# Five products of constants on the whole TensorE array, placed between the tasks of a recurrent-attention and MLP kernel

## The chip, the cores and the metric

One core of a Trainium2 chip runs the kernel. The metric is the device time of one execution in microseconds. The engines are TensorE (PE; its weight loads are listed apart as PEld), VectorE (DVE), ScalarE (ACT), GpSimd (POOL), and SyncE (SP), which issues the transfers. Each works through its own queue of instructions in order and waits on semaphores for the others.

## What is computed

The input is six arrays of 4 batches, 8 heads, 768 time steps and 40 channels. A recurrent state of 40 by 40 per batch and head is read and updated step by step; the outputs of all heads are put side by side and go through an MLP with a gated activation.

```python
for t in range(S):
    y[:, :, t] = einsum('bhd,bhde->bhe', r_t, state)
    Sa = einsum('bhde,bhe->bhd', state, a_t)
    state = state * w_t[:, :, None, :] - einsum('bhd,bhe->bhde', Sa, b_t)
    state = state + einsum('bhd,bhe->bhde', v_t, k_t)
x = y.transpose(0, 2, 1, 3).reshape(3072, 320)
h = x @ w_in                                # 320 -> 2048
out = (h * sigmoid(1.702 * h)) @ w_out      # 2048 -> 320
```

## The kernel before

The 768 steps are cut into 12 chunks of 64, and the 4 batches into 2 pairs. One chunk of one pair is a **unit**; there are 24, numbered from 0. Units 0 and 1 are the first chunk of the two pairs, 2 and 3 the second, and so on. Within a chunk the recurrence is solved as a triangular system, so that nearly all work is matrix products. For each unit the code makes these stages:

- `decay`: logarithms of w are summed by two products into `ps_cum` and `ps_cumc` (in the first four units), and ScalarE takes exponentials of them (FT, GT, wch, G).
- `prep`: the inputs are scaled by these; two products give the scores `ps_A` and `ps_RV`, which VectorE masks into A and RV.
- `inverse`: one product gives the scores `ps_N`; then five levels double the inverse of a triangular block. In the first four units this is `plain_level`: TensorE makes `ps_level` from EX and PT (40 instructions, the last eight with the identity tile `ident`), ScalarE or VectorE copies it into PT (L784), VectorE transposes it into EX (L723), and the next level takes both. After the last level come T (L707), `ps_Q`, and `ps_T`, which fill in the lower block.
- `solve`: from unit 2 on the carried state is turned over (`ps_zT`) and read (`ps_rz`); `ps_B` collects the known side, `ps_X` applies the inverse, VectorE masks it into M (L907), and `ps_y` adds the products of RV with kh and of M with bh: alternating groups of eight instructions, 64 in all. The result goes out to memory and comes back turned (`x_dram`, `xT_all`) for the MLP.
- `mlp`, one for each chunk (both pairs): `up` tasks into `ps_up`, an activation into g, `down` tasks into `ps_down`. The weights are put together from pieces in the first 75 us (L447 to L463).

Nearly all products work on a quarter of the 128x128 array (64 rows by 64 columns). Four such products run side by side on the four quarters, and each float32 product is two weight loads and two matmul instructions in the profile. All are recorded by the helper `mm` at L300.

Every step is a task. `Plan.add` records which tasks it must follow; the order of all tasks on all engines is written out by hand in the string `ORDER` and put into effect by `listed`. A token names a task by number, engine (p TensorE, a ScalarE, d VectorE, g GpSimd, s SyncE), and for those that use PSUM the bank pair 0 to 3. A tile in PSUM is made by `psum` for the pair of the token; the tasks that share a tile form a chain, and the next tile on the same bank pair has to wait until the one before it has been read. The order of tokens of one engine is the order in its queue.

On TensorE the order around the change is this, with the tokens: unit 0's level 0 (107p0), its level 1 (110p3), ps_N and ps_RV of unit 1, further levels of units 0 and 1 mixed with ps_cum and ps_cumc of unit 2, unit 0's last level (119p3), unit 0's ps_Q (126p2), ps_N of unit 2, a level of unit 1, ps_T and ps_X of unit 0, unit 1's last level, unit 0's ps_y (136p1), unit 1's ps_Q (182p0), ps_B of unit 1, ps_A of unit 2, ps_T of unit 1, a level and ps_RV of unit 2, unit 1's ps_X (190p0), ps_cum and ps_cumc of unit 3 (334p1, 335p3), unit 1's ps_y (192p2), ps_zT of unit 2 (316p0), unit 2's level 1 (295p3), unit 3's ps_N (358p1), unit 2's level 2 (298p3), ps_rz of unit 2, ps_RV of unit 3, two levels, ps_zT, another level, ps_B, a level, ps_A, ps_cum, and then the first `up` tasks. From there on the tasks of later units stand between `up` and `down` tasks.

Of the kernel before, what the change touches and what calls it, by code (L numbers as in the profile page):

```python
# [108 lines left out]
4a 11s 132p0 104a1 105d1 142p2 26s 143p3 133a0 106d 130p1 14s 144a3 13s 107p0 15s 18s 151g 108a0 109d0 51s 131a1 110p3 27s  # L109
149g 150d 111a3 112d3 159p0 156p1 145a2 161d0 160a0 152g 113p3 345s 92a 162d 25s 153d 114a3 163p2 42s 115d3 34s 19a 274s 264p0  # L110
165d2 265p3 164a2 22d 266a3 166p2 20d 273s 21d 33s 43s 167a2 154p3 168d2 23g 35s 28a 157d1 116p2 155d3 169p1 117a2 118d2 267a0
279d 63s 280g 119p3 277s 171d1 36s 44s 123a3 120d3 343s 125d3 121a 278g 124d3 29d 287a 126p2 170a1 288p0 127a2 30d 172p1 122a3
31d 289a0 128p2 54s 173a1 129d2 32g 174d1 134p3 147s 37a 290d0 175p2 135d3 180a2 146s 178a2 275s 176d2 136p1 179a2 479s 38d
181a2 45s 39d 177a 282g 291d 91s 138a1 182p0 188p3 281d 183a0 186p2 139d 137a1 283p0 187a2 184p1 189a3 40d 276s 292p2 46a
284d0 41g 285p3 185d1 344s 148a 286d3 190p0 293a2 294d2 334p1 335p3 357a 140s 191d0 268g 336a3 315d 192p2 47d 337a1 348d 316p0
194a2 295p3 349d 61s 317a0 195g 60s 347s 358p1 296a3 62s 297d3 360d1 318a0 298p3 271a 361d 319p0 338g 300d3 196s 193a2 320a0
346s 355p2 385d 270s 48d 299a3 362p0 356d2 351g 301p3 363a0 364d0 350g 269s 141s 386p2 197s 302d3 365p0 387a2 352g 359a1 303d3
388a2 323p1 367d0 366a0 321p3 49d 324a1 304p2 322a3 478s 325d1 50g 353p0 309a2 470p3 354d0 209p1 307a2 210p1 310a2 305d2 211p1
308a2 272d 198p0 341a 199p0 72s 212p1 70s 64a 200p0 340s 368p2 52s 342d 339s 69s 201p0 369a2 202p0 370d2 203p0 471a 213p1 65d
214p1 389p2 66d 472a3 483g 204p0 390a2 560s 371p3 67d 306a 53s 215p1 71s 482s 216p1 372a3 217p1 476a 220p2 373d3 68g 218p1  # L120
221p2 477d 219a1 205p0 222p2 206p0 223p2 224p2 207p0 55a 311p3 225p2 79s 312d3 80s 226p2 208a0 58d 313p1 374p3 314d1 227p2 56d
379a3 228p2 229p2 57d 326p0 230a2 59g 393p1 327d0 378a3 391p2 394a1 375d3 231p0 558s 392d2 376a 232p0 233p0 395d1 559s 81s 73a
78s 234p0 480s 381p2 235p0 328p1 481s 382a2 74d 377a3 485d 380a3 236p0 75d 492a 242p2 486d 243p2 82a 76d 484d 77g 383p3 237p0
384d3 244p2 329d1 330d1 488p3 473d 238p0 531d 245p2 487g 246p2 489d3 85d 532p1 239p0 533a1 396p3 331d 332s 474s 475s 534a1
240p0 247p2 397d3 562s 241a0 535p1 83d 490p3 536a1 84d 398p0 572a 491d3 86g 550p1 555s 561s 253p3 399d0 551a 333s 400d0 254p3
401d 402s 554s 255p3 552a1 564d 493p0 705s 556a 567g 570p1 403s 494d0 248p2 563d 566g 249p2 495d0 498d 256p3 571d1 565g 250a2
496a0 251d2 252s 696p1 497g 557d 539p0 537p2 704s 257p3 538a2 540d0 258p3 553d 611d 697a 499d 573p2 784s 700s 259p3 576a2
574d2 710d 260p3 541d0 575d2 404p0 578d 261a3 577g 405p0 579d 698a1 568p2 711g 500p1 406p0 569d2 501a1 407p0 262d3 263s 708s
580p2 702a 502d1 408p0 582d2 409p0 503d 410p0 583d 504a 612p3 411p0 584g 613d3 412p0 614d3 413p0 505p1 709d 414a0 426p3 506d1
427p3 428p3 507d1 429p3 699d 581d2 430p3 615p1 785s 706s 701s 703d 431p3 616a1 585p0 432p3 508d 586a0 433p3 587d0 434p3 509a  # L130
588d 435p3 589d 448p2 436a3 510p1 590p0 511a1 449p2 592d0 591a0 512d1 415p3 513d 416p3 593d 514a 417p3 594g 418p3 515p0 419p3
516a0 517d0 595p1 518d 420p3 596a1 597d1 421p3 598d 422p3 519a 599d 423p3 424p3 520p0 425a3 437p1 521d0 438p1 523d0 522g 439p1
524d0 440p1 525d0 441p1 442p1 526d0 527p3 718p0 929s 528a3 443p1 719d0 787s 444p1 720d0 529p3 445p1 721d0 446p1 530d3 600p0
723d 447a1 542p3 722d 724g 603d0 605a0 619p1 604d0 543d3 450p2 620a1 606d0 544p3 621d1 601d0 602d 617p1 707s 546d3 451p2 618a1
783s 712d 547g 713d 607p0 725p1 608a0 452p2 609p0 453p2 548s 610d0 932s 454p2 727d1 726d1 622p0 728d 545d3 729a 775p1 455p2
623d0 780s 776a 549s 756d 730p3 624p0 456d2 457d2 731d3 458s 459p2 777a1 778g 732d3 786s 788g 781a 779s 626d0 460p2 625d0 627g
733d 795p1 835d 734a 461p2 735p3 791g 462p2 628s 736a3 796d1 737d3 716p0 792g 738d 463p2 782d 739g 1011s 920p1 757p3 925s
464p2 717d0 758a3 629s 759a3 790d 465p2 740p0 789d 466p2 741a0 742d0 921a 797p3 467d2 760p0 1008s 468d2 800a3 923d 652p2 469s
761d0 922a1 653p2 926a 930s 798d3 714p1 799d3 654p2 924s 802d 801g 655p2 934d 803a 656p2 836p0 657p2 715d1 658p2 659p2 837d0
762p3 838d0 927d 660p2 763a3 661p2 764p1 662a2 743d 630p0 744d 928s 631p0 632p0 765d1 804p3 766d1 633p0 805a3 806d3 634p0 807d  # L140
635p0 808a 745p2 636p0 748d2 637p0 749d2 839p1 933g 750d2 638p0 840a1 1009s 751d2 639p0 809p3 746d2 935g 640a0 641p1 810d3
642p1 793p2 747a 811d3 674p0 812d 794d2 813a 752p3 643p1 753a3 814p2 644p1 815a2 816d2 754p3 645p1 755d3 646p1 817d 647p1 818a
767p2 841p3 768d2 648p1 842a3 649p1 819p2 650p1 820a2 821d2 675p0 769p3 822d 651a1 823d 771d3 931s 770d3 772g 824p2 936d 676p0
827a2 828a2 942p1 829a2 677p0 1153s 830a2 937d 945a1 773s 663p3 825d2 664p3 943d1 1156s 826a 665p3 944d1 999p2 947d 946g 666p3
1000a 1004s 980d 940p1 948g 667p3 941d1 668p3 774s 669p3 670p3 831p1 671p3 1001a2 1002d 1003s 832d1 672p3 1005a 1013d 678p0
673a3 1006d 833p2 843p1 679p0 834d2 1007s 844d1 938p2 845d1 680p0 939d2 846p3 681p0 847d3 949p1 1012g 682d0 848p2 950a1 683d0
1014d 684s 685p3 849d2 1015g 1010s 850d2 1021p0 1016g 951d1 686p3 1024a0 1232s 851d 1235s 981p2 687p3 982a2 952d 852s 1022d0
983a2 953g 1144p1 1023d0 688p3 1026d 1145a 1149s 1025d 1027g 984p2 1059d 689p3 1154s 954p0 853s 985a2 1147g 690p3 1158d 1148s
955a0 956d0 986p2 1146a1 957d 1150a 691p3 958d 987a2 1151d 988p0 692p3 989a0 1152s 990d0 959p1 693a3 865p2 960a1 694d3 866p2
961d1 867p2 695s 962d 868p2 963d 1028p0 869p2 1029a0 1030d0 870p2 1031d 1157g 871p2 1159d 1032a 1060p3 872p2 873p2 1061a3  # L150
874p2 1062d3 1033p1 875a2 854p0 1035d1 855p0 1036d 856p0 1037d 1063p3 857p0 1064d3 1034a1 858p0 964p2 859p0 965a2 966d2 1038p1
# [97 lines left out]
def rwkv7_gelu_quick(ctx: ExitStack, tc: tile.TileContext, time_d, v_d, w_d, wc_d, ak_d, b_d, rv_d, w_in, w_out, out):  # L249
# [93 lines left out]
    ident = single("ident", [128, 64])  # L343
# [689 lines left out]
    for i in range(NU):  # L1033
# [10 lines left out]
        if i % 2:  # L1044
            mlp(i // 2)
# [84 lines left out]
```

## Time and profile before

| | us |
|---|---|
| runs shown, median (lowest to highest) | 678.83 (678.51 to 679.16) |
| the profiled execution's own time | 678.87 |
| its span in the profile | 677.2 |
| TensorE busy | 650.6 |
| VectorE, ScalarE, GpSimd busy | 447.1, 330.6, 175.0 |
| mean granted clock of TensorE | 0.989 |

The profile is one execution. It is read by its page (busy time, the span in 40 slices, the chain of work that ended last, the costliest groups) and by views of the trace: the timeline, which lists runs of like instructions with start and length in us, the count behind an x, and in brackets the idle time of the engine before them with what ended it; the view of stretches, which gives for each stretch how long the engine was busy and the clock that TensorE was granted (1.00 is full); and the chain of waits, in order of time. "issue" as releaser means that the profile shows nothing that the engine waited for.

### The profile page before, as it was taken

What the parts mean: (1) busy time and instruction counts of PE and PEld (TensorE: products, weight loads), DVE (VectorE), ACT (ScalarE), POOL (GpSimd) and SP (SyncE); (2) the same over time, 40 slices, a digit from 0 to 9 for tenths busy, and PEclk for the clock granted to TensorE, in tenths of its full rate; (3) what the DMA queues carried; (4) which work ended last, traced back from release to release, by engine and by line L of the source; (5) the groups of instructions that cost most, each with busy time, mean ns of one, the idle gap of its engine ahead of it and who ended that gap; (6) DMA issues with size and microseconds to landing.
All of it is one profiled execution on the core that took longest, in us unless ns stands there. A gap on an engine that the chain in (4) does not pass through costs nothing.

```text
span 677.2 us, 42176 instructions
## 1 busy us (share of the span) xinstructions
PE 650.6 (96%) x19488; PEld 561.3 (83%) x19488; DVE 447.1 (66%) x906; ACT 330.6 (49%) x688; POOL 175.0 (26%) x204
## 2 busy tenths in 40 slices
PE   5668999999999999999999999999999999999997
PEld 5567887987987888898998898787988799899895
DVE  5686887777768668667776687868556766675001
ACT  4675955634664655554545435454454354252110
POOL 6442444224123023124123211321412321300000
PEclk9887999999999999999999999999999999999999
DMA  7883736315324224332304413513412412100100
GB/s 234 295 252 126 235 111 183 103 45 157 111 64 132 84 62 129 106 107 77 113 24 133 139 34 108 155 33 107 145 34 72 126 46 63 53 14 29 45 12 20
DMA packets 35311, 69.72 MB, mean 103 GB/s; under 512 B 5440, under 2 KB 14656, under 8 KB 35136
## 3 DMA queue, kind: packets, MB, share of 16 engines
q1 hardware_dynamic: 35136, 67.03, 32.6%
q8 instruction: 153, 2.51, 1.5%
q14 instruction: 22, 0.18, 0.1%
HBM read 59.15 MB, written 7.86 MB: 99 GB/s over the span
## 4 chain that ended last, share of the span: by engine, by line
PE 94%; ACT 2%; DVE 2%; issue 1%; DMA 1%; DVEq 0%; ACTq 0%; SPq 0%
PE ps_up L300 31%; PE ps_down L300 31%; PE ps_level L300 9%; PE ps_y L300 5%; PE ps_B L300 5%; PE ps_X L300 2%; PE ps_A L300 2%; PE ps_rz L300 2%; PE ps_N L300 2%; PE ps_RV L300 2%; PE ps_zT L300 1%; ACT PT L784 1%; PE ps_cum L300 1%; PE ps_Q L300 1%; PE ps_T L300 1%
## 5 line engine op out<-in xcount | busy, mean ns | idle before, releaser
L300 PE MATMUL ps_up<-xT_all,w_sb 64*64 64x256 f32 x3840 | 250.1, 377 | 0.4 <-PE ps_rz L300 0.2
L300 PE MATMUL ps_down<-w_sb,g 64*64 64x320 f32 x3072 | 239.5, 430 | 0.3 <-ACT zr L869 0.2
L300 PEld LDWEIGHTS ps_up<-xT_all,w_sb 64*64 64x64 f32 x3840 | 169.6, 133 | 15.3 <-issue 0.8
L300 PEld LDWEIGHTS ps_down<-w_sb,g 64*64 64x64 f32 x3072 | 133.3, 133 | 39.8 <-issue 1.3
L988 ACT ACTIVATE g<-ps_up 128x1024 f32<-128x1024 f32 x48 | 49.2, 1024 | 45.0 <-PE ps_up L300 44.6
L709 POOL TENSOR_TENSOR EX<-ES,quads 128x512 f32<-128x512 f32 x29 | 38.3, 1323 | 113.3 <-DVE ES L702 75.8
L751 ACT COPY W<-ps_level 128x512 f32<-128x512 f32 x56 | 32.7, 585 | 69.7 <-PE ps_level L300 68.0
L300 PEld LDWEIGHTS ps_level<-W,EX 64*64 64x64 f32 x2560 | 58.7, 134 | 5.8 <-DVE T L830 0.2
L300 PE MATMUL ps_level<-W,EX 64*64 64x64 f32 (+1 forms) x2560 | 55.9, 217 | 0.0
L753 DVE TENSOR_TENSOR E<-two,ps_level 128x256 f32<-128x256 f32 x80 | 33.2, 416 | 34.0 <-ACT W L751 30.3
L707 ACT ACTIVATE EX<-ES,quads 128x256 f32<-128x256 f32 x80 | 36.3, 501 | 30.5 <-DVE ES L702 29.9
L619 POOL TENSOR_TENSOR ak<-ak,FT 128x512 f32<-128x512 f32 x16 | 21.4, 1335 | 75.9 <-DMA ak<-in_ak 52.0
L300 PEld LDWEIGHTS ps_level<-PT,EX 64*64 64x64 f32 x1280 | 32.1, 146 | 8.8 <-DVE EX L723 5.7
L300 PE MATMUL ps_level<-PT,EX 64*64 64x64 f32 (+2 forms) x1280 | 34.2, 245 | 5.3 <-DVE EX L723 4.5
L702 DVE STREAM_TRANSPOSE ES<-E 128x256 f32<-128x256 f32 x80 | 35.3, 443 | 4.4
L300 PE MATMUL ps_y<-M,bh 64*64 64x104 f32 (+1 forms) x768 | 35.0, 247 | 2.4 <-issue 2.1
L300 PE MATMUL ps_y<-RV,kh 64*64 64x104 f32 (+1 forms) x768 | 34.8, 247 | 0.0
L891 ACT COPY B<-ps_B 128x416 f32<-128x416 f32 (+1 forms) x34 | 16.5, 491 | 33.8 <-PE ps_B L300 33.6
L300 PEld LDWEIGHTS ps_y<-RV,kh 64*64 64x64 f32 x768 | 28.5, 133 | 2.3 <-DVE M L907 0.5
L300 PEld LDWEIGHTS ps_y<-M,bh 64*64 64x64 f32 x768 | 27.2, 133 | 2.8 <-issue 2.3
L907 DVE TENSOR_TENSOR M<-ps_X,later 128x832 f32<-128x832 f32 (+1 forms) x24 | 23.8, 993 | 8.2 <-PE ps_X L300 8.0
L627 POOL TENSOR_TENSOR kh<-time,G 128x320 f32<-128x320 f32 x18 | 16.1, 892 | 48.5 <-PE ps_y L300 34.6
(131 smaller groups left out, 1092.9 us busy)
## 6 DMA issues: line engine op xcount, KB each, us to landing
ak<-in_ak SPq DMA_DIRECT2D x48, 160.0 KB
rv<-in_rv SPq DMA_DIRECT2D x48, 160.0 KB
time<-in_time SPq DMA_DIRECT2D x24, 320.0 KB
xT_all<-x_dram SPq DMA_DIRECT2D x48, 160.0 KB
wc<-in_wc SPq DMA_DIRECT2D x20, 264.0 KB
logw<-in_w SPq DMA_DIRECT2D x24, 160.0 KB
RV<-in_v SPq DMA_DIRECT2D x24, 160.0 KB
b<-in_b SPq DMA_DIRECT2D x48, 80.0 KB
```

The source lines that it names most:

```text
L300: nc.tensor.matmul(o, lhsT, rhs, start=start, stop=True, skip_group_check=True)
L619: plan.add(R, {"DVE": 690.0, "POOL": 1270.0, "sbuf": True}, lambda t: of(t.engine).tensor_mul(ahT(), ahT(), FT_of(i)), reads=T("ak", "FT") ...
L627: plan.add(R + 4, {"POOL": 870.0, "DVE": 490.0, "sbuf": True}, lambda t, n=n, dst=dst: of(t.engine).tensor_mul(dst(i)[:, :, :D], by_head(t ...
L702: plan.add(rank, dve(256), lambda t: nc.vector.transpose(ES(n), source(t)), writes=[key("ES", n, 6)], **reads)
L707: nc.scalar.activation(dst[:, :, h], ES(n), ACT.Copy, scale=quads[:, h, :1])
L709: of(t.engine).tensor_mul(dst, ES(n).unsqueeze(2).to_broadcast([128, 8, 2, 32]), quads.unsqueeze(1).to_broadcast([128, 8, 2, 32]))
L751: plan.add(rank, any2(512), lambda t: copy(t.engine)(tiles_of(W(n + 1)), blocks(psum(t, ""), 64)), writes=[key("W", n + 1, 5)], pair=pair)
L753: plan.add(rank, dve(256), lambda t: nc.vector.tensor_sub(tiles_of(E(n + 1)), every(two32, [128, 2, 4, 32]), blocks(psum(t, ""), 64)[:, :, ...
L784: plan.add(rank, any2(768), lambda t: copy(t.engine)(tiles_of(PT), blocks(psum(t, ""), 96)), writes=[("PV", turn(i, n + 1, 5))], pair=pair)
L891: plan.add(R, any2(4 * wide), lambda t: copy(t.engine)(dst(), some(psum(t, "")[:, :, :208])), writes=[("Bv", i)] if x and c > 0 else T("B" ...
L907: plan.add(R + 1, dve(8 * wide), lambda t: nc.vector.tensor_tensor(M_of(i)[:, :, :wide].rearrange("p (j b) n -> p b j n", b=2), some(psum( ...
L988: plan.add(-45, {"ACT": 1030.0, "table": "gelu"}, lambda t: nc.scalar.activation(g_of(c * NQ + q).rearrange("p m r n -> p r m n"), psum(t, ...
```

## The change

Five tasks are added, numbered 2700 to 2704. Each is one product on the whole array, 128 rows by 128 columns, of 512, 512, 512, 256 and 384 moving columns. The stationary operand is the first column of the constant tile `ident`, repeated 128 times; the moving operand is `ident` repeated along the columns. The result goes to a tile `ps_idle` of its own in the first half of a bank pair; no task reads it. No other task is altered, taken out or moved.

The code, and the five places in `ORDER`, which are shown here with one token to a line and the neighbours that matter (the string is wrapped anew behind the first insertion; all other tokens stand in the same order as before):

```diff
+    def keep_on(n, cols):
+        row, rows = ident[:, :1].to_broadcast([128, 128]), ident.unsqueeze(1).to_broadcast([128, cols // 64, 64])
+        plan.add(0, pe((0.25, cols)), lambda t: mm(psum(t, "ps_idle")[:, 0, :cols], row, rows, True), pair=("idle", n))
+    for n, cols in enumerate((512, 512, 512, 256, 384,)):
+        keep_on(n, cols)
     tasks = plan.listed(ORDER)
```

```diff
 107p0
...
 131a1
+2700p3
 110p3
...
 119p3
...
 287a
+2701p0
 126p2
...
 136p1
...
 138a1
+2702p3
 182p0
...
 190p0
...
 294d2
+2703p1
 334p1
...
 295p3
...
 347s
+2704p1
 358p1
```

On TensorE's queue the first product thus stands between unit 0's level 0 and level 1, the second between unit 0's last level and its ps_Q, the third between unit 0's ps_y and unit 1's ps_Q, the fourth between unit 1's ps_X and unit 3's ps_cum, and the fifth between unit 2's level 1 and unit 3's ps_N.

More of the change, by code (lines that the diff above doesn't have):

```diff
@@ L112 @@
[L112 to L115, printed above, removed]
```

269 lines of the change are left out of this document (137 added, 132 removed).

## The prediction

> **What bounds the kernel now.** I read the page first, for the engine that sets the end and for the clock it was granted.
>
> ```profile
> span 677.2 us, 42176 instructions
> PE 650.6 (96%) x19488; PEld 561.3 (83%) x19488; DVE 447.1 (66%) x906; ACT 330.6 (49%) x688; POOL 175.0 (26%) x204
> PEclk9887999999999999999999999999999999999999
> q8 instruction: 153, 2.51, 1.5%
> ```
>
> TensorE sets the end: 96% busy, and the only slices below full clock lie in the first tenth. The time to be had is there. So next came the view of stretches, cut where the clock changes. Its edges fall on a grid of 3.41 us (columns: length, TensorE busy, count, granted clock, DMA share, GB/s).
>
> ```profile
> 16.88:20.29 3.41, 1.71 (x79) 1.00 0.97 338
> 20.29:23.71 3.42, 3.35 (x97) 0.50 0.82 282
> 30.53:33.95 3.42, 1.82 (x84) 1.00 0.81 242
> 40.78:44.19 3.41, 1.34 (x61) 1.00 0.85 261
> 44.19:47.61 3.42, 3.33 (x103) 0.50 0.42 128
> 47.61:51.02 3.41, 2.51 (x114) 1.00 0.92 280
> 51.02:54.43 3.41, 2.69 (x128) 1.00 0.50 164
> 54.43:57.85 3.42, 1.70 (x78) 1.00 0.08 25
> 57.85:61.26 3.41, 2.96 (x88) 0.50 0.78 250
> 61.26:64.67 3.41, 3.41 (x96) 0.50 0.53 156
> 70.00:670.00 600.00, 599.17 (x17744) 1.00 0.30 90
> ```
>
> A stretch with 1.71, 1.34 or 1.70 us busy is followed by one at half clock; stretches with 1.82, 2.51 and 2.69 are not. So the clock is halved for the next 3.41 us when TensorE was busy for less than about half (1.7 to 1.8 us). It is halved three times: from 20.29, from 44.19, and for two stretches from 57.85. From 70 us on TensorE waits 0.83 us in 600, so what is won or lost before 70 us should come out at the end.
>
> Third, the timeline of TensorE around its waits (the bracket holds the wait and its releaser).
>
> ```profile
> 18.64 0.89 PE L300 MATMUL ps_level<-PT,EX 64*64 64x96 f32 x32 [1.70 <-DVE EX L723]
> 35.09 0.46 PE L300 MATMUL ps_Q<-T,P 64*64 64x64 f32 x16 [1.96 <-ACT T L707]
> 40.43 0.40 PE L300 MATMUL ps_y<-M,bh 64*64 64x104 f32 x5 [0.32 <-DVE M L907]
> 42.89 0.30 PE L300 MATMUL ps_y<-M,bh 64*64 64x104 f32 x2 [2.07 <-issue]
> 44.02 0.29 PE L300 MATMUL ps_Q<-T,P 64*64 64x64 f32 x5
> 46.94 0.37 PE L300 MATMUL ps_T<-QT,Tc 64*64 64x64 f32 x2
> 48.96 0.89 PE L300 MATMUL ps_X<-B,T 64*64 64x104 f32 x30
> 49.68 0.43 PE L300 MATMUL ps_cum<-logw,edges 64*64 64x160 f32 x2
> 51.67 0.36 PE L300 MATMUL ps_cum<-logw,edges 64*64 64x160 f32 x3 [1.55 <-issue]
> 53.84 0.52 PE L300 MATMUL ps_zT<-ident,zr 40*40 40x40 f32 x26
> 55.35 0.28 PE L300 MATMUL ps_zT<-ident,zr 40*40 40x40 f32 x6 [0.99 <-issue]
> 58.30 1.56 PE L300 MATMUL ps_level<-PT,EX 64*64 64x96 f32 x32 [1.25 <-DVE EX L723]
> ```
>
> There are two kinds of wait. Those of 1.70, 1.96 and 1.25 us are for another engine and stand between two tasks. Those of 2.07, 1.55 and 0.99 us are released by nothing and break off inside a task: ps_y of unit 0 after five of its products with M, ps_cum of unit 3 after two of eight, ps_zT of unit 2 after 26 of 32. I take them for waits for TensorE's own instructions: 2 x 19488 matmuls and weight loads over the 153 instruction packets are 255 a packet, and between the last two breaks the code issues 6 + 32 + 64 + 26 = 128 matmuls, 256 instructions. A packet's end is thus a place in the program where TensorE can be held however fast it ran before.
>
> **The change part by part.** It removes nothing. It adds five products of the identity tile, on the whole array, with 512, 512, 512, 256 and 384 columns: behind unit 0's first level, behind its last level, behind its ps_y, behind unit 1's ps_X, and behind unit 2's second level.
>
> No row shows a 128-row product. The nearest are four quarter-array products of 256 columns each (eight instructions).
>
> ```profile
> 69.59 3.24 PE L300 MATMUL ps_up<-xT_all,w_sb 64*64 64x256 f32 x56
> 72.62 0.29 PE L300 MATMUL ps_level<-PT,EX 64*64 64x96 f32 x4
> L300 PE MATMUL ps_up<-xT_all,w_sb 64*64 64x256 f32 x3840 | 250.1, 377 | 0.4 <-PE ps_rz L300 0.2
> ```
>
> 56 instructions in 72.62 - 69.59 = 3.03 us are 0.43 us for eight, the whole array used over 256 columns. If one full product takes the same, 512 columns cost 0.87 us, 384 cost 0.65, and the five 2176 / 256 x 0.43 = 3.7 us of TensorE at full clock, 7.4 at half. The low end is half of it, 1.8 us, if it goes in one instruction instead of two; the high end, with nothing overlapped, 2 x 0.377 us per 256 columns, 6.4 us. I take 3.7, because ps_up runs back to back like that.
>
> *First product.* It fills 0.87 us of the 1.70 us wait, so it delays nothing. The stretch from 16.88 gets 1.71 + 0.87 = 2.6 us busy, and the clock should stay up from 20.29. What that is worth is read from the chain and the wait behind it:
>
> ```profile
> 21.48 2.03 PE ps_level L300 x40
> 29.44 1.15 PE ps_level L300 x40
> 23.58 0.80 ACT L784 COPY PT<-ps_level 128x768 f32<-128x768 f32 x1 [0.81 <-PE ps_level L300]
> ```
>
> The same 40 instructions take 2.03 us at half and 1.15 at full clock: 0.88 less, of which the copy behind it can take up its 0.81 of waiting. Value: -0.8; ends 0 (the weight piece of the next activation, L447, has not landed earlier) and -0.9.
>
> *Second product.* 0.87 in a wait of 1.96: nothing. If all moved 0.8 us forward, the stretch from 30.53 would fall to about 1.1 us busy without it; it keeps what the first won.
>
> *Third and fourth product.* Neither stands in the wait that it is near. The 2.07 us lie inside ps_y; the third product comes after ps_y's last product, at 44.0, where ps_Q follows without a pause. The 1.55 us lie inside ps_cum, the fourth comes before it, directly behind ps_X. The third is 0.87 us on TensorE's path, 1.74 at half clock, and it comes too late to lift the stretch from 40.78 (1.34 us) unless the work before it is 0.4 us earlier. What hides it is the fetching: the next two packet ends are at 46.9 and 50.1, and 1.55 us of waiting follow. Also, 12 more instructions ahead put the packet's end 12 earlier, from ps_cum's fifth instruction (two products done, a third loaded) back past its start and into ps_X's last four products. ps_X then ends only after the fetch, and M waits for it:
>
> ```profile
> 50.42 0.98 DVE L907 TENSOR_TENSOR M<-ps_X,later 128x832 f32<-128x832 f32 x1
> ```
>
> M would start near 52.0 instead of 50.42 and hold ps_y's products with M until 53.0, 0.4 us later than now; the wait of 0.99 behind takes that. I put this place at +0.4: ends -0.3 (the stretch from 44.19 at full clock, its gain ending at the packet ends) and +1.7 (the third product at half clock with nothing to hide it).
>
> *Fifth product.* 0.65 us between a level and unit 3's ps_N, inside the 1.25 us wait that follows; ps_N comes later, but VectorE reads it only after the transpose that this wait is for. The stretch from 54.43 has 1.70 + 0.65 = 2.35 us busy, and the clock stays up from 57.85. There TensorE is its own bound:
>
> ```profile
> 58.30 1.98 PE ps_level L300 x40
> 60.28 0.85 PE ps_rz L300 x32
> 61.14 0.85 PE ps_RV L300 x32
> 61.99 3.19 PE ps_level L300 x80
> 57.53 0.72 DVE L723 STREAM_TRANSPOSE EX<-ps_level 128x512 f32<-128x512 f32 x1 [2.83 <-ACT PT L784]
> 65.37 0.92 DVE L784 COPY PT<-ps_level 128x768 f32<-128x768 f32 x1
> 65.50 0.89 PE L300 MATMUL ps_level<-PT,EX 64*64 64x96 f32 x32
> ```
>
> 58.30 to 64.67 at twice the clock saves 3.2 us at most. But the levels of two units wait for each other's copies (0.80 to 0.92) and transposes (0.72): followed task by task, unit 3's second level, now at 65.50, could start at 63.05, 2.4 us earlier. A packet (256 instructions) then goes in under 3 us, while it took 46.94 to 51.67, 4.7, and 51.67 to 55.35, 3.7, from packet end to packet end when TensorE was waiting for it with DMA busy. I take off 0.6 for that: -1.8, ends 0 and -3.2.
>
> The sum: -0.8 + 0.4 - 1.8 = -2.2. The profiled execution took 678.87 us (span 677.2, 1.7 around it), the median shown is 678.83: 678.87 - 2.2 = **676.7 us**.
>
> [...]
>
> **The rivals.**
>
> *The clock doesn't heed these products, slower.* Their operands are one column and an identity, nearly all zeros; if activity is counted otherwise than as busy time, all three halvings stay. Then the third product stands at 44.0 in a half-clock stretch, 1.74 us in front of unit 1's whole solution, with nothing won elsewhere: 680.5. It decides once the stretch behind 57.85 stays at 0.50. For it: no row shows such a product. Against: all stretches shown go by busy time.
>
> *The fetch takes the gain.* TensorE runs ahead into the packet ends at 46.9, 50.1 and near 60.4 and 64.6; the first product's 0.8 is lost in the 2.07 us wait, the last stretch keeps 1 us, the third product costs 0.4: 678.3. A form of it: faster work before 51.02 meets the wait sooner, that stretch falls under 1.7 us busy, and the clock halves one stretch later. For it the three breaks; against, the chain from 58.30 has none.
>
> *The grid isn't fixed to the start.* If it shifts from run to run, some runs of before had fewer halvings and the products find less to save: with the 0.8 and 1.8 there in a third of the cases, -0.9 + 0.4 = -0.5, 678.4, with scatter. [...] Against it: the runs of before lie within 678.51 to 679.16, 0.65 us, while the halvings cost more than that.
>
> *All of it.* Full clock in all four half-clock stretches with little fetch wait: -0.9 - 0.3 - 3.2 = -4.4, 674.5.
>
> **How the numbers follow.** Forecast 0.42, products not heeded 0.20, fetch 0.20, moving grid 0.10, all of it 0.08. The forecast's own range is 675.6 to 677.8. The range of 8 in 10 runs from 674.9 (into the largest case) to 680.3 (into the slower case). This kernel's measurement tells 0.2%, 1.4 us, from no change. Faster, below 677.5: 0.42 x 0.9 + 0.08 + a quarter of fetch and grid = 0.54. Slower, above 680.2: most of 0.20 and a little of the rest, 0.19. Within: 0.27.
>
> **What would show it.** Right, step by step: the stretch from 20.29 at 1.00; the level there 1.15 long; the fetch break inside ps_X instead of ps_cum; the stretch from 57.85 at 1.00, and the first ps_up at 69.59 - 2.2 = 67.4 us. The third product should start within 0.1 us of ps_y's end, with no wait ahead of it. Wrong: 0.50 still standing from 57.85, new halvings after 51.02, the products much longer than 0.9 us per 512 columns, or a first ps_up near 67.4 with a span that is unchanged, since then TensorE would have had waits to spare after 70 us.

## The result and the profile after

Over 22 runs of each on one chip the changed kernel takes 681.67 us in the median (676.49 to 686.37), the kernel before 678.22 (673.87 to 679.21). The ratio is 1.006, its 95% interval 1.0043 to 1.0076: slower, by 4.1 us. (The ratios here and below are not the quotients of the medians beside them; the quotients of the means differ from them by up to 0.001. The means of this comparison lie 4.3 us apart, the medians 3.45.) The runs of both scatter far more than the three shown of before. The profiled execution of the changed kernel took 685.11 us, in the upper part of its runs. It is one execution; what other profiles show beside it is said below.

The page of the changed kernel, the lines that answer to those of before:

```profile
span 683.5 us, 42197 instructions
PE 654.2 (96%) x19498; PEld 560.3 (82%) x19498; DVE 445.9 (65%) x906; ACT 331.1 (48%) x688; POOL 174.8 (26%) x204
PEclk9989999999999999999999999999999999999999
q8 instruction: 153, 2.51, 1.5%
```

The clock is higher than before (9989 for 9887), and the time is longer all the same. The view of stretches of the changed kernel, TensorE alone (stretch, length, busy, matmuls, granted clock, DMA share, GB/s):

```profile
17.20:20.60 3.40, 2.74 (x99) 1.00 0.96 325
20.60:24.00 3.40, 2.31 (x102) 1.00 0.94 331
41.10:44.50 3.40, 1.30 (x60) 1.00 0.88 229
44.50:47.90 3.40, 2.83 (x57) 0.50 0.15 53
47.90:51.30 3.40, 3.40 (x46) 0.50 0.46 144
54.70:58.10 3.40, 2.09 (x60) 1.00 0.18 68
58.10:61.50 3.40, 2.56 (x132) 1.00 0.02 5
70.00:670.00 600.00, 597.67 (x17833) 1.00 0.30 90
```

The first and the last halving of before are gone, as forecast: 2.74 us busy from 17.20, and full clock behind it; 2.09 and 2.56 from 54.70, and full clock there too. One pair of half-clock stretches is left, behind 1.30 us busy from 41.10. The wait that empties that stretch stands in TensorE's timeline of the changed kernel (start, length, what, count, and in brackets the wait before it with its releaser; the change moves all lines of the code behind it, so that L300 is L301 here):

```profile
16.99 1.20 PE L301 MATMUL ps_idle<-ident 128*128 128x512 f32 x2
25.43 0.33 PE L301 MATMUL ps_cumc<-edges,logw 64*64 64x65 f32 x2 [0.23 <-issue]
32.41 0.63 PE L301 MATMUL ps_level<-PT,EX 64*64 64x96 f32 x18 [2.20 <-issue]
33.95 1.12 PE L301 MATMUL ps_idle<-ident 128*128 128x512 f32 x2
35.95 0.46 PE L301 MATMUL ps_Q<-T,P 64*64 64x64 f32 x16 [0.87 <-ACT T L708]
38.56 0.64 PE L301 MATMUL ps_level<-PT,EX 64*64 64x96 f32 x20 [1.16 <-issue]
45.08 0.62 PE L301 MATMUL ps_y<-M,bh 64*64 64x104 f32 x8 [2.67 <-DVE w_sb L452]
47.71 2.07 PE L301 MATMUL ps_idle<-ident 128*128 128x512 f32 x2
55.86 0.40 PE L301 MATMUL ps_X<-B,T 64*64 64x104 f32 x4 [1.32 <-issue]
56.19 0.70 PE L301 MATMUL ps_idle<-ident 128*128 128x256 f32 x2
60.46 0.36 PE L301 MATMUL ps_zT<-ident,zr 40*40 40x40 f32 x15 [0.84 <-issue]
61.67 0.91 PE L301 MATMUL ps_idle<-ident 128*128 128x384 f32 x2
68.85 0.46 PE L301 MATMUL ps_level<-PT,EX 64*64 64x96 f32 x10 [1.28 <-issue]
72.24 0.48 PE L301 MATMUL ps_B<-RV,A 64*64 64x104 f32 x10 [0.43 <-issue]
74.38 1.46 PE L301 MATMUL ps_up<-xT_all,w_sb 64*64 64x256 f32 x18
76.16 2.17 PE L301 MATMUL ps_up<-xT_all,w_sb 64*64 64x256 f32 x35 [0.32 <-issue]
```

Before, three waits had no releaser (2.07, 1.55 and 0.99 us). Here, up to 76 us, they are 0.23, 2.20, 1.16, 1.32, 0.84, 1.28, 0.43 and 0.32. None of the five products has a wait ahead of it in this profile, so they don't wait for their banks in PSUM. The 2.67 us ahead of ps_y are one more of them, though the profile names a releaser; VectorE's timeline of the same kernel tells why:

```profile
41.66 1.01 DVE L908 TENSOR_TENSOR M<-ps_X,later 128x832 f32<-128x832 f32 x1
43.56 0.78 DVE L452 TENSOR_SCALAR w_sb<-w_sb 128x1280 f32<-128x1280 f32 x1
```

The tile that these products read, M, is there at 42.67. The operation named works on a weight piece that ps_y does not read; it only happens to end at 44.34, the last one before TensorE goes on. From the break at 38.56 to here TensorE went through 31 matmuls of that level, 16 of ps_T, 32 of ps_X, 40 of a level and 8 of ps_y: 127, which with their weight loads are 254 instructions, and with two semaphore instructions of TensorE's queue 256. By this count it is an instruction packet's end, and a transfer on the instruction queue ends 1.48 us before 45.08 (table further down). The first ps_up starts at 74.38, 4.8 us later than before. From 70 to 670 us TensorE waits for 2.33 us where it was 0.83; most of the additional waits lie ahead of 90 us (1.21 us from 70 to 90, where before had none). The span is longer by 6.3 us, and nearly all of that is lost ahead of 90 us.

### The profile page after: what moved, and what is told of

The parts are those of the page before. It is cut to its first block, busy times and chain, and to the rows that moved or that the text cites. A ratio compares the mean times of both kernels' runs of the same rounds, so it can differ in the third digit from the quotient of the medians.

```text
span 683.5 us, 42197 instructions
## 1 busy us (share of the span) xinstructions
PE 654.2 (96%) x19498; PEld 560.3 (82%) x19498; DVE 445.9 (65%) x906; ACT 331.1 (48%) x688; POOL 174.8 (26%) x204
## 3 DMA queue, kind: packets, MB, share of 16 engines
q8 instruction: 153, 2.51, 1.5%
## 4 chain that ended last, share of the span: by engine, by line
PE 94%; issue 2%; DVE 2%; ACT 1%; DMA 1%; DVEq 0%; SPq 0%; ACTq 0%
PE ps_up L301 30%; PE ps_down L301 30%; PE ps_level L301 9%; PE ps_y L301 5%; PE ps_B L301 5%; PE ps_X L301 3%; PE ps_N L301 2%; PE ps_rz L301 2%; PE ps_RV L301 1%; PE ps_A L301 1%; PE ps_zT L301 1%; PE ps_cum L301 1%; PE ps_Q L301 1%; PE ps_T L301 1%; DMA b<-in_b 1%
## 5 line engine op out<-in xcount | busy, mean ns | idle before, releaser
L301 PE MATMUL ps_up<-xT_all,w_sb 64*64 64x256 f32 x3840 | 250.6, 377 | 0.5 <-issue 0.3
L301 PE MATMUL ps_down<-w_sb,g 64*64 64x320 f32 x3072 | 240.6, 430 | 0.2 <-ACT zr L870 0.2
L301 PEld LDWEIGHTS ps_up<-xT_all,w_sb 64*64 64x64 f32 x3840 | 169.3, 133 | 16.0 <-issue 0.8
L301 PEld LDWEIGHTS ps_down<-w_sb,g 64*64 64x64 f32 x3072 | 134.5, 133 | 39.1 <-issue 0.7
L301 PEld LDWEIGHTS ps_level<-W,EX 64*64 64x64 f32 x2560 | 58.5, 134 | 6.1 <-DVE T L831 0.2
L301 PE MATMUL ps_level<-W,EX 64*64 64x64 f32 (+1 forms) x2560 | 55.7, 217 | 0.0
L301 PE MATMUL ps_level<-PT,EX 64*64 64x64 f32 (+2 forms) x1280 | 32.8, 233 | 7.6 <-issue 4.6
L301 PEld LDWEIGHTS ps_level<-PT,EX 64*64 64x64 f32 x1280 | 30.3, 136 | 12.0 <-issue 5.2
L301 PE MATMUL ps_y<-M,bh 64*64 64x104 f32 (+1 forms) x768 | 35.3, 252 | 3.3 <-DVE w_sb L452 2.7
L301 PE MATMUL ps_y<-RV,kh 64*64 64x104 f32 (+1 forms) x768 | 35.1, 251 | 0.0
L301 PEld LDWEIGHTS ps_y<-RV,kh 64*64 64x64 f32 x768 | 28.3, 136 | 2.3 <-DVE M L908 0.5
L301 PEld LDWEIGHTS ps_y<-M,bh 64*64 64x64 f32 x768 | 26.8, 137 | 3.7 <-DVE w_sb L452 2.9
L301 PE MATMUL ps_B<-RV,A 64*64 64x104 f32 (+1 forms) x768 | 28.7, 257 | 0.4 <-issue 0.4
```

Of the source, the lines that this page charges most:

```text
L301: nc.tensor.matmul(o, lhsT, rhs, start=start, stop=True, skip_group_check=True)
```

## The experiments

Three theories were on record before the first runs. **A**: the products' own TensorE time stands in its way. **B**: instruction packets end elsewhere, and TensorE meets their fetching sooner. **C**: the halvings of the clock were only moved. All ratios below are against runs of the kernel before on the same chip, with 95% intervals; 12 runs of each kernel unless another number is given. The clocks are means over those runs. Each of the four groups ran on a chip of its own. The kernel before has medians of 678.2 to 682.0 us in the five comparisons, so that profiles of different groups can't be compared by their length.

### Width, and single products

Five products of 64 columns at the five places; all but the third, with 2702p3 taken out; the first alone; the third alone. The four lines stand in this order.

```diff
-    for n, cols in enumerate((512, 512, 512, 256, 384,)):
+    for n, cols in enumerate((64, 64, 64, 64, 64,)): 
+    for n, cols in enumerate((512, 512, 256, 384,)):
+    for n, cols in enumerate((512,)):
+    for n, cols in enumerate((512,)):
```

> All five products at their places, each cut to 64 columns: the instruction packets end where they do in the changed kernel, but the products take under 0.1 us each and hardly count as busy. Theory A (the products' own time on TensorE's path, about 2.0 + 0.64 + 0.85 us of the chain): back to before, ratio 0.999 to 1.001. Theory B (the packets' ends moved, and TensorE waits longer for the fetches): still slower, ratio 1.004 or more. Theory C (the clock: halvings moved): three stretches at half clock as before, ratio near 1.000.

> The changed kernel without its third product (512 columns behind unit 0's ps_y). Theory A: the 2.0 us that it takes in the chain go, ratio 1.003 instead of 1.006. Theory B: the next packet end takes it up, ratio stays 1.005 to 1.006.

> The first product alone (512 columns in the wait behind unit 0's first level). Theory A and the prediction: it costs nothing and keeps the clock up from 20.29, ratio 0.9985 to 0.999. Theory B: the 0.7 us won until 29 us are lost at the packet end in unit 1's third level, where a wait of 1 to 2 us stands on issue, ratio 1.000 to 1.002.

> The third product alone. Theory A: it stands at half clock in front of unit 1's ps_Q with nothing to hide it, +1.7 to +2.0 us, ratio 1.0025 to 1.003. Theory B: the wait for the next packet shrinks by part of it, ratio 1.000 to 1.001.

| | median us | ratio | mean clock |
|---|---|---|---|
| kernel before (35 runs) | 681.46 | | 0.988 |
| five of 64 columns | 684.87 | 1.0041 (1.0012 to 1.007) | 0.992 |
| without the third | 683.63 | 1.0031 (1.0005 to 1.0057) | 0.993 |
| first alone | 681.99 | 1.0008 (0.9982 to 1.0034) | 0.987 |
| third alone | 682.27 | 1.0011 (0.9982 to 1.004) | 0.989 |

The five narrow products lose 0.41%, where the wide ones lost 0.6% in the first comparison. From the timeline of the kernel with the five narrow ones:

```profile
43.68 0.43 PE L301 MATMUL ps_idle<-ident 128*128 128x64 f32 x2
47.93 0.39 PE L301 MATMUL ps_A<-ak 40*64 40x64 f32 x10 [2.12 <-issue]
53.28 0.40 PE L301 MATMUL ps_X<-B,T 64*64 64x104 f32 x4 [1.08 <-issue]
57.61 0.36 PE L301 MATMUL ps_zT<-ident,zr 40*40 40x40 f32 x15 [0.84 <-issue]
```

The third takes 0.43 us (under 0.1 was expected), where the wide one took 2.07 at half clock, and most of the loss stays. A had forecast 0.999 to 1.001 for them, B 1.004 or more. So the TensorE time of the products is not the main cause: A falls in its simple form. The run without the third speaks the other way: 1.003 is what A forecast, while B's 1.005 to 1.006 lies at the upper edge of its interval. The breaks at ps_X and ps_zT are where the changed kernel has them (x4 and x15), since the five add the same 20 instructions. The single products are not told from nothing. The first alone doesn't raise the mean clock either, 0.987 for 0.988.

### Moving the packets' ends without the products

The changed kernel again; the kernel before with 5 quarter-array products of 64 columns (20 instructions, as many as the five products) behind unit 0's first ps_cumc, or with 64 of them (256 instructions, a whole packet); and the changed kernel with 59 of them, so that products and these together are 256.

```diff
+    def filler(n):
+        def go(t):
+            for k in range(n):
+                r, h = QUARTERS[k % 4]
+                mm(psum(t, "ps_pad")[HALF[h], r, :64], ident[HALF[r]], ident[HALF[r], :64], True)
+        plan.add(0, pe((n / 4, 64)), go, pair=("pad", 0))
+    filler(5)
...
-87p0 88p1 24s
+87p0 88p1 2700p3 24s
```

> The changed kernel again, beside the three that follow, since the time of the kernel before differs from chip to chip. All theories: ratio 1.004 to 1.008.

> The kernel before with five quarter-array products (20 instructions, together some 0.1 us) in the wait of TensorE between 5.4 and 6.6 us: nothing but a shift of all later packet ends by as many instructions as the change adds. Theory B (the packets' ends, in the whole program): slower, ratio 1.002 to 1.005. Theories A and C (path of the products, clock): no difference, ratio 0.999 to 1.001.

> The kernel before with 64 such products (256 instructions, one packet, 1.9 us of TensorE in the same wait of 1 to 2 us and the next). Every later packet end falls again where it fell before. Theory B: ratio 0.999 to 1.001, at most 1 us from the start being delayed. If any added instructions cost the time: slower than the shift by 20.

> The changed kernel with 59 quarter-array products ahead (236 instructions): behind its fifth product the packet ends fall where they fell before. Theory B: the loss behind 70 us goes (2 us and more), ratio 0.999 to 1.003, with the products' own 2.0 us of the third still there. Theory A: ratio 1.005 or more, as for the changed kernel.

| | median us | ratio | mean clock |
|---|---|---|---|
| kernel before (35 runs) | 680.65 | | 0.988 |
| changed kernel | 684.21 | 1.0036 (1.0002 to 1.0069) | 0.996 |
| 20 instructions more | 681.74 | 1.000 (0.9969 to 1.0031) | 0.991 |
| 256 instructions more | 683.41 | 1.0022 (0.9994 to 1.0049) | 0.985 |
| products, and 256 in all | 685.24 | 1.0051 (1.0024 to 1.0078) | 0.988 |

Two things follow. C falls for the changed kernel: its clock is 0.996 here and 0.996 over the 22 runs of the first comparison (0.990 to 1.000). An estimate from the mean clocks, with 1.00 and 0.50 as the clocks that the views of stretches show: at 0.988, 2 x 0.012 x 679 = 16 us of a run go at half clock; at 0.996 it is 5.4. By it the products take away two thirds of the half-clock time, and the time grows. And where the packets end isn't it alone: shifting all ends by 20 is not shown to cost anything, and shifting them back onto the places of before (256 in all) doesn't bring the time back. B had forecast 1.002 to 1.005 for the shift by 20 and 0.999 to 1.003 for the last kernel; A had forecast 1.005 or more for the last, and that came. B as it stood on record is not borne out by these two. In the last kernel the clock is 0.988, as before, with all five products at their places. Five of the quarter-array products take 0.67 us as a row, 64 of them 3.65, where 0.1 and 1.9 were expected.

The stretches at half clock lie elsewhere in nearly every profile. With 20 instructions more there was one, from 42.9 us, with 256 more there were stretches from 12.1, 32.6 and 59.9. In the second profile of the changed kernel the third product takes 1.12 us, from 44.35 on, where it took 2.07 at half clock in the first. So the halvings of before's profile were one draw.

### The same kernels with light transfers

The raw weights come in by 32 transfers of 320 KB, 10.5 MB in all; 19 of them, 6.2 MB, are issued in the first 45 us. Here each is cut to 16 columns (16 KB), in the kernel before and in the changed one. On the same chip ran two kernels with full transfers: one with the first and fifth product (512 and 384 columns), one with the second and fourth (512 and 256).

```diff
-            plan.add(rank, {"SP": 350.0}, lambda t, some=some: nc.sync.dma_start(raw()[:, some], src[:, some]),
+            plan.add(rank, {"SP": 350.0}, lambda t, some=slice(some.start, some.start + 16): nc.sync.dma_start(raw()[:, some], src[:, some]),
...
+        fixed = lambda dt: ident.bitcast(dt)[:, :1].to_broadcast([128, PIECE])
...
-            nc.scalar.activation(scale().bitcast(FP32), word(FP32, 1), ACT.Prelu, scale=2.0 ** -112, alpha=2.0 ** 32)
+            nc.scalar.activation(scale().bitcast(FP32), fixed(FP32), ACT.Prelu, scale=2.0 ** -112, alpha=2.0 ** 32)
...
-            nc.vector.tensor_single_scalar(word(INT32, 1), word(UINT32, 0), 2.0 ** -29, op=ALU.mult)
+            nc.vector.tensor_single_scalar(word(INT32, 1), fixed(UINT32), 2.0 ** -29, op=ALU.mult)
```

> The kernel before, with each of the 32 transfers of weight pieces cut to 16 of its columns and the two operations that read them reading a constant column instead: the weights, and so the output, are not the reference's, all instructions on the engines stay. It is the base for the next run; only the difference of the two counts. Theory B (an instruction packet's fetch, begun late while the transfers fill the queues, takes back what TensorE wins and more): with the transfers gone this kernel waits less for its instructions in the first 60 us, start of a fetch some 0.7 us behind the packet's end as after 70 us, and is 1 to 4 us faster than before. Theory A (the products stand in TensorE's way by themselves): no expectation here beyond 0 to 4 us faster.

> The changed kernel with the same lightened transfers. Theory B: the loss against the lightened kernel before vanishes, the difference of the two lies between -2 and +1 us. Theory A: each of the five places costs as with full transfers, the difference stays at +3 to +4 us, as between the changed kernel and before (0.36 to 0.6%).

> Only the first (512 columns) and the fifth product (384), the two that were to win. If the cost of the five is spread evenly over their places: two fifths of 3.7 us, +1.5 us, 0.2%. If the loss is bound to the third and fourth place, where the packet ends fall into ps_y and ps_X: 0 or a gain, down to the -2.6 us that the prediction gave these two.

> Only the second (512) and the fourth product (256). Spread evenly: +1.5 us, 0.2%. If the fourth place, just ahead of unit 3's sums and with nothing to hide it, carries the loss: +2 us or more. If the first and the fifth carry it: 0 within 0.8 us.

| | median us | ratio | mean clock |
|---|---|---|---|
| kernel before (32 runs) | 680.61 | | 0.989 |
| before, light (10 runs) | 678.43 | 0.9942 (0.9919 to 0.9966) | 0.994 |
| changed, light (11 runs) | 678.28 | 0.9951 (0.9932 to 0.9971) | 0.999 |
| first and fifth | 681.96 | 1.0007 (0.9984 to 1.0031) | 0.989 |
| second and fourth | 681.54 | 0.9995 (0.9974 to 1.0016) | 0.995 |

With the transfers out of the way the five products, at their full widths and places, cost 0.7 us by the means of the runs (678.23 and 677.50), give or take 1.4 (twice the standard error of the difference, 0.72). A had forecast +3 to +4 us here, B -2 to +1. With full transfers the same step cost, by the means, 4.3 us (give or take 1.3) in the first comparison and 2.9 (give or take 1.9) in the second, that of the changed kernel again; the changed kernel with full transfers did not run beside these. The fall from 4.3 to 0.7 is clear of the scatter, that from 2.9 is not. By the first comparison the greater part of the loss hangs on the early transfers. The view of stretches, TensorE alone, of before, of the changed kernel, of before with light transfers, and of the changed one with light transfers:

```profile
10.00:45.00 35.00, 23.93 (x832) 0.94 0.89 286
0.00:70.00 70.00, 49.15 (x1720) 0.90 0.71 222
```

```profile
10.00:45.00 35.00, 22.81 (x748) 0.99 0.93 286
45.00:70.00 25.00, 21.04 (x700) 0.87 0.43 136
0.00:70.00 70.00, 47.98 (x1552) 0.95 0.71 219
```

```profile
10.00:45.00 35.00, 25.08 (x840) 0.85 0.43 127
45.00:70.00 25.00, 20.70 (x849) 1.00 0.38 111
0.00:70.00 70.00, 49.92 (x1781) 0.93 0.44 130
```

```profile
10.00:45.00 35.00, 27.90 (x974) 1.00 0.45 131
45.00:70.00 25.00, 21.13 (x714) 0.93 0.39 102
0.00:70.00 70.00, 53.17 (x1792) 0.98 0.45 130
```

The count of matmuls between 10 and 45 us says it. Under load (DMA share 0.89 and 0.93) the changed kernel does 748 for 832, at a clock of 0.99 for 0.94. Without the load it does 974 for 840: there the products do what they were forecast to do, and by 45 us TensorE is a packet, 134 matmuls, ahead. By 70 us the two are level, 1792 and 1781. In the changed kernel with light transfers the first wait of over half a us that has no releaser begins at 49.9 us, at a packet whose fetch began 2.7 us late. It leaves 1.74 us busy in the stretch up to 53.22, and the next one goes at half clock. So most of the lead is gone at 60 us. These are its waits:

```profile
51.60 0.36 PE L301 MATMUL ps_zT<-ident,zr 40*40 40x40 f32 x15 [1.67 <-issue]
60.03 0.46 PE L301 MATMUL ps_level<-PT,EX 64*64 64x96 f32 x10 [0.36 <-issue]
63.69 0.48 PE L301 MATMUL ps_B<-RV,A 64*64 64x104 f32 x10 [0.71 <-issue]
67.61 2.17 PE L301 MATMUL ps_up<-xT_all,w_sb 64*64 64x256 f32 x35 [0.33 <-issue]
```

and in the kernel before with light transfers:

```profile
60.51 0.24 PE L300 MATMUL ps_level<-PT,EX 64*64 64x96 f32 x1 [0.82 <-issue]
64.17 0.25 PE L300 MATMUL ps_B<-RV,A 64*64 64x104 f32 x1 [0.80 <-issue]
68.16 1.73 PE L300 MATMUL ps_up<-xT_all,w_sb 64*64 64x256 f32 x26 [0.20 <-issue]
```

At the break at 60.03 the changed kernel is 0.5 us ahead (60.51), and from there both go at the pace of the packets. From break to break there is one packet: 63.69 - 60.03 = 3.66 us and 3.92 in the one, 3.66 and 3.99 in the other. Up to 49.9 us none of the waits of the changed kernel under load (2.20, 1.16, 2.67) has its like here. The records of the transfers on the instruction queue, set beside TensorE's instructions, give the parts of such a break; one line for each packet, in us. I take the packet that is fetched for the one behind the next end, where TensorE goes on, since in no line does it go on sooner than 1.35 us after the transfer's end:

```
                   TensorE passes    next packet's      its transfer   TensorE goes on
                   the packet's end  transfer begins    takes          after its end by
before                  26.61          +0.74              1.38           +1.91
                        30.64          +0.59              1.47           +3.69
                        36.38          +3.94              1.09           +1.48
changed                 25.42          +4.23              1.26           +1.49
                        32.41          +3.71              1.09           +1.35
                        38.56          +3.82              1.22           +1.48
changed, light          23.82          +0.85              0.98           +3.10
                        28.75          +0.55              1.15           +3.99
                        34.42          +1.39              1.13           +1.66
                        38.61          +0.83              1.41           +2.03
```

Where the last column is 1.35 to 1.49, TensorE had waited just before (2.07 us in before's profile, 2.20, 1.16 and 2.67 in the changed kernel's): I read it as held until the fetch was through. Where it is larger, it was still busy. Under load four of the six fetches began 3.7 to 4.2 us late, the other two 0.59 and 0.74; with light transfers they began 0.55 to 1.39 late. In these profiles the kernel before meets so late a fetch once in its three packets, the changed one three times in a row, and each then takes 6.1 to 7.0 us from end to end. There the packets set the pace, and the higher clock (0.99 for 0.94 from 10 to 45 us) only brought TensorE to the end of the first one sooner, at 25.42 for 26.61.

The profiles of the other kernels bear out the load and not the loss. Of the packet ends passed between 20 and 45 us, the latest fetch begins 3.0 to 4.6 us late in each of the 15 profiles with full transfers, and 1.3 to 2.2 in the three with light ones. But among the 15 are kernels that lose nothing that can be told. With 20 instructions more, in an execution of 678.29 us, two fetches begin 3.5 and 4.5 us late, and TensorE waits for both packets:

```profile
29.64 0.79 PE L300 MATMUL ps_level<-PT,EX 64*64 64x96 f32 x25 [0.87 <-issue]
41.60 0.31 PE L300 MATMUL ps_y<-RV,kh 64*64 64x104 f32 x3 [3.38 <-issue]
```

So late fetches alone don't make an execution long. That the latest of them begins later with full transfers is seen in these profiles (3.0 to 4.6 us for 1.3 to 2.2); that they make the loss, and not another effect of the load, is not shown.

The two halves of the change, first with fifth and second with fourth, are not told from nothing. They add up to less than the five: 1.0 us by the means, 2.0 to either side. Against the 2.9 us of the second comparison that doesn't exclude a plain sum, against the 4.3 of the first it does. Their clocks are not what the prediction had: the first and fifth, which were to keep the clock up, leave it at 0.989; the second and fourth raise it to 0.995.

### Is the gain to be had, and does before pay for its load?

The first and fifth product with light transfers; then, with all data read, the kernel before with three transfers of weight pieces issued later (51s, 54s, 63s), with five (42s and 43s too), and the changed kernel with three.

```diff
-15s 18s 151g 108a0 109d0 51s 131a1
+15s 18s 151g 108a0 109d0 131a1
...
+51s 54s 52s
...
+63s 61s
...
+42s 43s 44s
```

> The lightened transfers again, with the first and the fifth product only, which stand in waits of TensorE. Lightened kernel before: 0.9942 of before. If a higher clock is worth time as soon as the fetches begin in time, this one is 1 to 3 us faster than that, 0.990 to 0.993. If the waits between the engines and the fetch cycles take the gain also without the load, 0.994 within 0.002.

> The kernel before with three transfers of weight pieces, 0.98 MB, issued later on SP's queue: two of the four quarters of the fifth piece, used at 82 us, issued at 18 and 35 us till now, and one of the sixth, issued at 31 us, each put beside the other quarters of its piece. Nothing else moves. If the load of the early transfers costs the kernel before its time (lightened: 7.8 of the 10.5 MB and more gone, -3.5 us), a tenth of it gives -0.3 to -0.5 us, hardly to be told from nothing; a loss of over 1 us would speak against.

> As m1_later, and two quarters of the fourth piece too, put behind on SP's queue beside its third. By the load: -0.5 to -1 us. The piece is used before 70 us; if it then comes too late for the first up products, +1 us or more.

> The changed kernel with the transfers of m1_later moved. Theory B (the load delays the fetches that the faster TensorE now waits for): it loses less than the changed kernel's 0.36 to 0.6%, 0.2 to 0.4%. Theory A: no difference to the changed kernel.

| | median us | ratio | mean clock |
|---|---|---|---|
| kernel before (35 runs) | 681.97 | | 0.989 |
| first and fifth, light | 678.41 | 0.9957 (0.9932 to 0.9981) | 0.996 |
| three transfers later | 683.16 | 1.0037 (1.0006 to 1.0068) | 0.989 |
| five transfers later | 684.20 | 1.0035 (1.0009 to 1.0061) | 0.989 |
| changed, three later (11 runs) | 684.01 | 1.0046 (1.0016 to 1.0076) | 0.995 |

With light transfers the two products that stand in waits show no gain over the light kernel before (0.9957 for 0.9942, on another chip): the second answer of the expectation. The moves lost 0.4% instead of winning a little; 1 us was the loss that would speak against the load as the price of the kernel before, and by the means the first move lost 2.2. So the amount of early transfers isn't all: which transfer stands ahead of which matters too. It may be the inputs that then come late; the chain of waits of the kernel with three moved goes through two such transfers up to 19 us, and so do that of the kernel with five products of 64 columns and that of the second comparison's changed kernel, while before's has one, up to 9.75, and none behind it. Start and length, from the kernel with the narrow five:

```profile
9.18 7.26 DMA ak<-in_ak
16.45 3.78 DMA RV<-in_v
```

They end at 20 us and the first product begins at 16, so the products hardly cause them. On this order of transfers the five products add 0.0009 (1.0046 against 1.0037), but with 0.35% to either side; that it is less than on the order of before is not shown. The changed kernel with three moved lies in the range of the changed kernel itself, which was A's forecast; B's 0.2 to 0.4% is not excluded.

**Open** remain the size of the loss and its sharing out: why five products cost 0.4 to 0.6% when the pairs and the single ones cost nothing that can be told, and how much of it is late fetches, how much late inputs and how much something else. None of these versions beats the kernel before while reading all its weights.

## Why the prediction was wrong

The forecast was 676.7 us, 2.2 below before; the kernel is 4.1 us above before. By its steps:

*What bounds the kernel: half right.* TensorE's waits without a releaser fit waits for instructions, at packets of 256: in the changed kernel's trace 256 instructions lie from 25.42 to 32.41 and again from there to 38.56, and at both places TensorE goes on 1.3 to 1.5 us after a transfer on the instruction queue. The break forecast inside ps_X's last four products stands exactly there, at 55.86, x4, and M follows it. The prediction's reading, that a stretch with less than 1.7 to 1.8 us busy halves the next one, fits the stretches of this profile that are shown above: 1.30 us, and 0.50 behind it, while 2.09 and more kept the clock. Over the 18 profiles it has exceptions to both sides (last section). It says nothing of the second stretch of a pair: before, 2.96 us busy at half clock from 57.85 were followed by half clock again, here 2.83 from 44.50.

*The step that failed* is the sentence that what is won before 70 us should come out at the end, with the two terms that rest on it, -0.8 and -1.8. The kernel with the first and fifth product alone tests them: -2.6 us would be 0.9962, and it measured 1.0007 (0.9984 to 1.0031). The clock that these terms rest on was not raised there in the mean, 0.989 as before; with light transfers it was, 0.996 for 0.994, and no gain showed either. A gain on the path of one stretch was carried to the end of the kernel as a gain of the same size. In the changed kernel's profile TensorE passes a packet's end 1.2 us earlier than before (25.42 for 26.61), and the next one 1.8 us later (32.41 for 30.64): between them the fetch began 4.23 us late. The prediction took such a delay for a fixed place in the program; in the profiles the same three ends have 4.23, 3.71 and 3.82 us in the changed kernel and 0.85, 0.55 and 1.39 in the one with light transfers. The changed kernel is 2.2 us behind at 45.08, and 4.8 at the next end, near 51.7 for 46.9, behind two half-clock stretches and the third product. A lead at 70 us need not reach the end either: the kernel before with light transfers starts its first ps_up at 66.03, 3.6 us earlier than before, and its span is 677.2 us as well (on another chip, so this is a hint and no proof). Why the five lose time, and don't only fail to win it, stays open; the runs show that the loss is not told from nothing with light transfers (0.7 us, give or take 1.4).

*First product: right in this profile, not in the mean.* The clock stays up from 20.60, and the forecast's 0.8 us are won for a while: the level that the prediction quotes at 29.44 starts at 28.78 in the chain. It is gone at the next packet's end, the 2.20 us wait. But over 12 runs this product alone has a clock of 0.987, and before has 0.988. An explanation would be that the stretches lie elsewhere from profile to profile, so that a product at a fixed place in the program meets the right one only now and then; that is not shown.

*Second product: right.* It lies in the wait for T, of which 0.87 us is left.

*Third and fourth product: mis-sized.* The term was +0.4 us. The third takes 2.00 us of the chain at half clock, the fourth 0.64:

```profile
47.78 2.00 PE ps_idle L301 x2
56.26 0.64 PE ps_idle L301 x2
61.74 0.85 PE ps_idle L301 x2
```

The high end of +1.7 was nearer for the profiled execution. But the five narrow products, 0.43 us in the third's row, lose 0.41%, and the third alone costs 1.0011 (0.9982 to 1.004), so it is not shown that the loss sits here.

*Fifth product: the clock right in this profile, the gain not there.* The clock was up from 58.10, and 1.8 us were to be won. The product itself stands in the chain with 0.85 us, and the work behind it goes by packets: from 60.46 to 76.16 four packets, 3.9 us each in the changed kernel (8.39 for two, 3.39, 3.92), 3.7 to 4.0 with light transfers. The prediction took off 0.6 us, for packets that TensorE could go through in under 3 us; at 3.9 for each of four, nothing is left of the 1.8: by the same count of instructions the four packets took 15.7 us here and 15.8 before (55.35 to 71.11), where two stretches among them went at half clock. The first ps_up, forecast at 67.4, starts at 74.38.

*The price of a product* was worked out as 0.87 us for 512 columns from quarter-array rows; a row takes 1.12 to 1.20 at full clock (256: 0.70, 384: 0.91, 64: 0.43).

*The rivals.* "The fetch takes the gain" had the mechanism, with 0.20 and 678.3 us; it let the fetch take back what was won and not more. That the fetch makes the loss is not shown either, as said above. Its form, that faster work meets the wait sooner and the next stretch falls under half busy, is what the profile shows at 41.10 (1.30 us busy, then half clock). "The grid isn't fixed to the start" was right as a fact: half clock began at 44.19 us in before's profile, at 44.50 in the changed kernel's and at 42.9 in that with 20 instructions more, which don't lie on one grid of 3.41 us counted from the start of the span, and with 256 more it came from 12.1, 32.6 and 59.9. The runs of before spread over 5 us, so that three runs within 0.65 us were too few to argue from. "The clock doesn't heed these products" fell for the five together: it rose from 0.988 to 0.996, with operands that are nearly all zeros. The first and fifth alone left it as it was.

## What to carry to other kernels

A gain in one stretch need not reach the end: before it is carried there, count the instructions to the next packet's end (256 to a packet in these profiles) and look whether the transfers are full there. Where a stage is paced by something late, test by lightening that thing in both kernels, old and new, and compare the two differences, all on the same chip. A cause read from a long execution has to be looked for in a short one too: here the late fetches were there as well. And a few runs that agree are no measure of the scatter: 22 runs here spread eight times as wide as the three shown.

## What the hardware showed that was not expected

- Clock and time went apart: with the products the granted clock rose from 0.988 to 0.996 and the time rose by 0.4 to 0.6%. Within a kernel, over the 326 runs of the experiments, a higher clock goes with a shorter time (correlation -0.45, 0.25 us for each 0.001).
- TensorE's instructions came in packets of 256: so many lie between its breaks, and the page has 153 packets, 2.51 MB, for 2 x 19488 matmuls and weight loads. With full transfers (DMA share about 0.9 from 10 to 45 us in before and in the changed kernel) the next transfer began up to 4.6 us after TensorE passed a packet's end; where it began 3.7 to 4.2 us late, a packet took 6.1 to 7.0 us. From 60.46 to 76.16 us in the changed kernel (DMA share 0.37) four packets took 8.39 (two of them), 3.39 and 3.92, and with light transfers it was 3.66 to 3.99 from break to break.
- A product on the whole array with 64 columns took 0.43 us as a row, one with 256 columns 0.70, with 384 0.91 and with 512 1.12 to 1.20 at full clock: from 256 on some 0.21 us more for each 128 columns.
- In the 18 profiles, one of each kernel, up to 110 us, 31 full-clock stretches of 3.41 us were followed by half clock. 29 of them had 1.75 us busy or less, the others 1.90 and 2.08; eight with 1.49 to 1.73 kept the clock. A stretch at half clock was followed by another if it had 2.72 us busy or less, and by full clock from 3.36 on; between these both came.
